# Low parts of eight weight tiles of an MLP made on TensorE instead of VectorE

## The chip, the cores and the metric

The kernel runs on one core of one Trainium2 chip. A core has TensorE (PE: matrix products, with weight loads shown apart as PEld), VectorE (DVE), ScalarE (ACT), GpSimd (POOL) and SyncE (SP), which starts most DMAs. The metric is device time of one execution in microseconds (us).

## The reference

What is computed, in the reference's own words, cut to what matters:

```python
out_up    = np.repeat(softmax_attention(q_d, k_d, v_d), 4, axis=2)   # on means of 4 positions
out_local = softmax(scale * q @ k.T within |i - j| < 4) @ v          # 4 batches, 8 heads, 576 x 64
x = (out_up + out_local) as 2304 tokens x 512
h = x @ w_in;  g = np.maximum(0.01 * h, h);  x = g @ w_out           # first MLP, 512 -> 2048 -> 512
h = x @ w_in2                                                        # second MLP, same sizes
g = where(h >= 1, h, where(h <= -1, 0, (h + 1)**2 / 4));  out = g @ w_out2
```

Weights come with more bits than one 16-bit number holds, and the output has to be as exact as float32.

## The kernel before

**Numbers in two parts.** Each matrix of the MLPs is held as two fp16 matrices, a high part (`hi`) and a low part (`lo`, what the rounding to `hi` left over). A product of two such matrices is three fp16 products (hi·hi, hi·lo, lo·hi) into one PSUM bank.

**Weights.** `weight(m, which, f, due)` prepares one tile of 128x512 of MLP `m` (`which` 0 is `w_in`, 1 is `w_out`; `f` counts 16 tiles of each). A DMA brings the tile; three VectorE operations (`c1`, `c2`, `c3`, lines 611, 617 and 623) put its fp32 words together; ScalarE writes `hi` as fp16, scaled by 256 (line 645); one VectorE operation at line 678 writes `lo` = 256·w − `hi`. Two other ways of making `lo` stand in the code: on TensorE for tiles below `LO_PE` (both zero here, so for none), and by DMA (also none).

**Attention.** It runs ahead of and between the first blocks of the first MLP, until about 140 us, on all engines. Its small fp32 products on TensorE use a part of the 128x128 array each: lines 1118 and 1268 use 64 columns, in pairs of which one writes PSUM partitions 0 to 63 and the other 64 to 127. One fp32 product of the program stands as two MATMUL records in the trace.

**The MLPs.** `stage(m, b)` goes over blocks of 512 or 256 tokens. For a block of 512 tokens one step is 12 products of 128x512 for `h` (`g1`, line 1627), the activation on ScalarE and VectorE (lines 1739, 1763, 1767), and 12 products for the output (`g2`, line 1788 for the first MLP, 1800 for the second). Three blocks of the second MLP use a scheme with fewer products (lines 1656 and 1726). A step needs `w_ready` of its tiles: both parts of the weights.

**What sets the order.** Nothing is scheduled on the chip. `Issue.run` is a planner that runs while the program is built: it gives each operation a cost, keeps a clock, and writes the instructions of each engine in the order in which its plan starts them; each engine then runs its own list in that order. Where the plan leaves TensorE with nothing to do in its first 140 us, `fill` (line 1994) writes in a product of a tile of zeros whose result nobody reads. Such filler products are in the program and are carried out whether or not TensorE would in fact have been idle. A changed cost or operation anywhere in the first 140 us so moves many instructions on every engine, as well as the number of fillers.

Of the kernel before, what the change touches and what calls it, by code (L numbers as in the profile page):

```python
# [56 lines left out]
LO_DMA = {1: (99, 99), 2: (99, 99)}  # L57


LO_PE = (0, 0)  # L60
ADD_PE = ()
PEAK_D = 4500
RESERVE = 2000
# [277 lines left out]
def kernel(  # L341
# [11 lines left out]
    nc = tc.nc  # L353
# [51 lines left out]
    banks = Banks([psum.tile([P, 512], F32, name=f"bank{i}") for i in range(8)])  # L405
# [9 lines left out]
    def t_act(n, psum_src=False, more=0):  # L415
        return (0.051 if psum_src else 0.093) + n / 1200.0 + 0.094 * more
# [9 lines left out]
    def t_mm(n):  # L426
        return 0.003 + n / 2400.0
# [17 lines left out]
    ident_w = const.tile([P, P], F32, name="ident_w")  # L445
    ident_n = const.tile([P, P], F16, name="ident_n")
# [111 lines left out]
    def weight(m, which, f, due):  # L558
        st = {}
        hi, lo = (e[:, f] for e in (w_in, w_out)[which][m])  # L560
        if which == 0:
            hi, lo = (e.rearrange("p c n -> p (c n)") for e in (hi, lo))
# [7 lines left out]
        if second:  # L570
            st = w_two[m, f - 1]
# [75 lines left out]
        free = (lambda: st["f", f].free(),)  # L647
        if m == 1 and f < LO_PE[which]:

            def low():  # L650
                ps = st["ps"] = banks.get()
                nc.tensor.matmul(ps, ident_w, st["f", f].ap, start=True, stop=False)
                nc.tensor.matmul(ps, ident_n, hi, start=False, stop=True)

            ch.op("PE", dict(dur=5 * t_mm(512), cols=5 * 512), low, banks=1, mlp=True,
                  after=free)
            w_ready[m, which, f] = ch.op(
                "ACT", t_act(512, True), lambda: nc.scalar.copy(lo, st["ps"]),
                after=(lambda: banks.put(st["ps"]),))
            ch.close()  # L660
            return
        if LO_DMA[m][0] <= f < LO_DMA[m][1]:

            def neg():
# [6 lines left out]
                after=(lambda: st["n"].free(),))  # L671
# [8 lines left out]
            after=free)  # L680
# [1285 lines left out]
    for m in (1, 2):  # L1966
        b0 = [e[1] for e in ORDER if e[0] == m][0]
        for f in range(KFF):
            i = step_of[m, b0, f // per_step(b0)]
            weight(m, 0, f, i)  # L1970
            weight(m, 1, f, i + 1.5)
# [58 lines left out]
```

## Time and profile before

| | |
|---|---|
| two executions that were timed | 848.5 and 848.83 us (median 848.66) |
| profiled execution, first to last instruction | 847.3 us |
| PE busy | 839.0 us (99%), 5446 MATMUL records |
| DVE busy | 640.7 us (76%) |
| ACT busy | 418.8 us (49%) |
| chain that ended last | PE 97% |

The profiled execution's own time is its span of 847.3 us; the timed ones are 1.2 to 1.5 us longer, which is what lies around the first and last instruction. A MATMUL's record lasts longer than the time until the next one may start (379 ns against some 216 ns for 128x512 fp16), since products overlap in the array; starts, not busy time, tell how fast TensorE goes. Some MATMUL records are missing, so the weight loads (LDWEIGHTS) are the better count.

### The profile page before, as it was taken

Reading aid. Unit: us, or ns where it says so; the run is one execution under the profiler, and the core shown is the slowest. Engines: PE = TensorE matmul, PEld = TensorE weight load, DVE = VectorE, ACT = ScalarE, POOL = GpSimd, SP = SyncE. Lnnn points to the kernel's source line nnn. Section 1 sums busy time; section 2 is a strip of 40 time slices with the busy share of each in tenths; the row PEclk is TensorE's granted clock in tenths of the full one; section 3 lists DMA queues with packets and bytes.
Section 4 is the critical chain, followed back from the end, with each engine's and each line's share of the span. In section 5 each row is a group of like instructions: output and inputs, shape, how many; then the busy total and the mean of one; then the engine's idle time right before and its main releaser. Section 6 shows DMA issues by size and latency. Waiting matters only on the chain.

```text
span 847.3 us, 14367 instructions
## 1 busy us (share of the span) xinstructions
PE 839.0 (99%) x5446; PEld 465.9 (55%) x5458; DVE 640.7 (76%) x1179; ACT 418.8 (49%) x1013; POOL 43.7 (5%) x64
## 2 busy tenths in 40 slices
PE   9999999999999999999999999999999999999997
PEld 5765554444444444444444444444688666666674
DVE  5997999899999899649969989997752446333442
ACT  4888765444444334544444324344533545544553
POOL 2101000000000031100500000000000000000000
PEclk9999999999999999999999999999999999999999
DMA  7779455457720353321842120000000000100010
GB/s 145 167 185 257 154 200 199 149 163 241 197 108 1 110 87 56 79 69 58 134 106 77 54 60 1 0 2 1 1 2 1 1 1 1 50 1 2 1 51 26
DMA packets 76675, 67.76 MB, mean 80 GB/s; under 512 B 36286, under 2 KB 62782, under 8 KB 76606
## 3 DMA queue, kind: packets, MB, share of 16 engines
q1 hardware_dynamic: 65406, 62.69, 25.6%
q0 software_dynamic: 11200, 4.15, 4.3%
q8 instruction: 43, 0.70, 0.4%
q14 instruction: 26, 0.21, 0.1%
HBM read 62.08 MB, written 4.72 MB: 79 GB/s over the span
## 4 chain that ended last, share of the span: by engine, by line
PE 97%; DVE 1%; ACT 1%; issue 0%; ACTq 0%; DVEq 0%
PE bank L1627 32%; PE bank L1788 22%; PE bank L1726 12%; PE bank L1656 11%; PE bank L1800 10%; PE bank L1994 2%; PE bank L923 1%; PE bank L1100 1%; PE bank L1118 1%; PE bank L1049 1%; PE bank L1208 1%; PE bank L1268 1%; PE bank L1251 1%; PE bank L1484 1%; ACT w L1226 0%
## 5 line engine op out<-in xcount | busy, mean ns | idle before, releaser
L1627 PE MATMUL bank<-arena,w 128*128 128x512 f16 (+1 forms) x1344 | 285.6, 364 | 0.0
L1627 PEld LDWEIGHTS <-w 128*128 128x128 f16 x1344 | 130.2, 98 | 135.0 <-issue 1.6
L1788 PE MATMUL bank<-arena,w 128*128 128x512 f16 (+1 forms) x960 | 198.5, 358 | 0.0
L1788 PEld LDWEIGHTS <-w 128*128 128x128 f16 x960 | 93.1, 98 | 88.4 <-issue 0.2
L1767 DVE SCALAR_TENSOR_TENSOR arena<-arena 128x512 f16<-128x512 f32 x144 | 98.9, 687 | 55.5 <-ACT arena L1763 53.9
L1763 ACT ACTIVATE arena<-arena 128x512 f16<-128x512 f32 x144 | 90.6, 629 | 53.7 <-DVE arena L1751 50.2
L1726 PE MATMUL bank<-w,arena 128*128 128x512 f16 x480 | 115.4, 379 | 0.1
L1743 ACT ACTIVATE arena<-bank,half 128x512 f32<-128x512 f32 x72 | 49.5, 687 | 87.3 <-DVE bank L1706 44.4
L1800 PE MATMUL bank<-w,arena 128*128 128x512 f16 x384 | 88.2, 379 | 0.0
L1739 ACT ACTIVATE arena<-bank 128x512 f32<-128x512 f32 x72 | 42.7, 593 | 91.2 <-PE bank L1627 91.0
L1751 DVE SCALAR_TENSOR_TENSOR arena<-arena,bank 128x512 f32<-128x512 f32 x72 | 49.1, 683 | 44.7 <-ACT arena L1747 44.6
L1726 PEld LDWEIGHTS <-arena 128*128 128x128 f16 x480 | 46.2, 98 | 41.7 <-DVE arena L1767 0.6
L1656 PE MATMUL bank<-arena,w 128*128 128x256 f16 (+1 forms) x576 | 62.1, 255 | 0.4 <-DVE bank L1699 0.4
L1800 PEld LDWEIGHTS <-arena 128*128 128x128 f16 x384 | 36.9, 98 | 43.2 <-issue 1.2
L1656 PEld LDWEIGHTS <-w 128*128 128x128 f16 x576 | 49.1, 98 | 13.0 <-issue 0.7
L1656 PE MATMUL bank<-arena 128*128 128x256 f16 (+1 forms) x432 | 46.0, 255 | 0.0
L1747 ACT ACTIVATE arena<-arena 128x512 f32<-128x512 f32 x72 | 45.1, 626 | 1.3
L1656 PEld LDWEIGHTS <-arena 128*128 128x128 f16 x432 | 36.9, 98 | 10.5
L1478 DVE TENSOR_TENSOR arena<-arena 128x768 f32<-128x768 f32 (+2 forms) x60 | 41.2, 688 | 1.4
L1403 DVE TENSOR_TENSOR arena<-arena 128x1792 f32<-128x1792 f32 x20 | 40.3, 2018 | 0.3 <-issue 0.3
L1448 DVE TENSOR_TENSOR arena<-arena 128x1792 f32<-128x1792 f32 x20 | 40.3, 2017 | 0.0
L1411 DVE TENSOR_REDUCE arena<-arena 128x28 f32<-128x1792 f32 x20 | 40.1, 2011 | 0.1
(146 smaller groups left out, 878.1 us busy)
## 6 DMA issues: line engine op xcount, KB each, us to landing
arena<-in_moe_w_in_dram SPq DMA_DIRECT2D x18, 512.0 KB
arena<-in_moe_w_out_dram SPq DMA_DIRECT2D x17, 512.0 KB
w<-in_moe_w_out_dram SPq DMA_DIRECT2D x15, 512.0 KB
out_dram<-arena SPq DMA_DIRECT2D x18, 256.0 KB
arena<-in_moe_w_in_dram SPq DMA_DIRECT2D x4, 1024.0 KB
w<-in_moe_w_in_dram SPq DMA_DIRECT2D x3, 1024.0 KB
arena<-in_k_dram SPq DMA_DIRECT2D x23, 112.0 KB
arena<-in_v_dram SPq DMA_DIRECT2D x23, 112.0 KB
```

Source lines behind the costliest of these rows:

```text
L1478: nc.vector.tensor_tensor(out, x, y, op=ALU.add)
L1627: nc.tensor.matmul(h[:, e], a[:, f, c, :], y[:, :, c, :], start=(n == 0), stop=(n == 3 * KDM - 1),)
L1656: nc.tensor.matmul(o[:, e], a[:, i, c], y[:, k, c, :], start=first and e == 0 and n == 0, stop=n == 5, skip_group_check=True,)
L1726: nc.tensor.matmul(st["acc"][t * NACC // 2 + k], a, y[:, f, :], start=(p == j == e == n == 0), stop=(p == PH - 1 and j == 1 and e == E - 1 ...
L1739: nc.scalar.activation(out=t, in_=st["h", p], func=AF.Prelu, scale=s_in * sg, alpha=0.01)
L1743: nc.scalar.activation(out=t, in_=st["h", p], func=AF.Relu, scale=0.5 * s_in, bias=half)
L1747: nc.scalar.activation(out=t, in_=t, func=AF.Square, scale=s_in ** -0.5)
L1751: nc.vector.scalar_tensor_tensor(out=t, in0=t, scalar=1.0 / s_in, in1=st["h", p], op0=ALU.min, op1=ALU.max)
L1763: nc.scalar.activation(out=gv(p)[0], in_=st["t", p].ap, func=AF.Copy, scale=so)
L1767: nc.vector.scalar_tensor_tensor(out=lo, in0=st["t", p].ap, scalar=so, in1=hi, op0=ALU.mult, op1=ALU.subtract)
L1788: nc.tensor.matmul(o, a, y[:, e, :], start=(first and n == 0 and c % E == 0), stop=(last and n == 2), skip_group_check=True,)
L1800: nc.tensor.matmul(st["acc"][tt], a, y[:, f, :], start=(first and n == 0), stop=(last and n == 2),)
```

## The change

For tiles `f` below 4 of both `w_in` and `w_out` of the first MLP, eight of its 32 tiles, the VectorE operation at line 678 is gone. In its place come, for each of them: two fp32 products of 64 columns of the array each (256·identity times the assembled fp32 words, 512 columns moving), one fp16 product of the full array (−identity times `hi`) that is added in the same bank, and a ScalarE copy of the bank to `lo` as fp16. The dictionary key with `f` keeps the banks of two tiles apart that share `st`.

```diff
-LO_PE = (0, 0)
+LO_PE = (4, 4)
...
             def low():
-                ps = st["ps"] = banks.get()
-                nc.tensor.matmul(ps, ident_w, st["f", f].ap, start=True, stop=False)
-                nc.tensor.matmul(ps, ident_n, hi, start=False, stop=True)
+                ps = st["ps", f] = banks.get()
+                for par in range(2):
+                    pp = slice(par * 64, (par + 1) * 64)
+                    nc.tensor.matmul(
+                        ps[pp], ident_w[:, pp], st["f", f].ap, start=True, stop=False,
+                        skip_group_check=True,
+                    )
+                nc.tensor.matmul(ps, ident_n, hi, start=False, stop=True, skip_group_check=True)
 
             ch.op("PE", dict(dur=5 * t_mm(512), cols=5 * 512), low, banks=1, mlp=True,
                   after=free)
             w_ready[m, which, f] = ch.op(
-                "ACT", t_act(512, True), lambda: nc.scalar.copy(lo, st["ps"]),
-                after=(lambda: banks.put(st["ps"]),))
+                "ACT", t_act(512, True), lambda: nc.scalar.copy(lo, st["ps", f]),
+                after=(lambda: banks.put(st["ps", f]),))
```

The planner writes a new order. From line 666 on, a line's number is 5 higher in the changed kernel. Over the whole program TensorE's list has the eight groups more (lines 654 and 658), and the filler stands 81 times in it instead of 86; all other operations stand as often as before, on every engine. The 81 fillers and the eight groups lie in the stretch of the attention, but the order of the MLPs' steps against each other differs here and there until the end.

TensorE, where the first of the eight groups stands (`ident` is an identity for transposes, `zeros` the filler's tile, `w_61` the room of the second MLP's weights, which serves as a buffer until they come, `w_81` the first MLP's weights). Before:

```order
L1268 MATMUL bank_66<-w_61 64x64 x2
L1268 MATMUL bank_70<-w_61 64x64 x2
L1994 LDWEIGHTS zeros
L1994 MATMUL bank_63<-zeros 128x512
L1100 MATMUL bank_64<-ident,w_61 72x72 x4
L923 MATMUL bank_67<-ident,w_61 128x64 x5
L1100 MATMUL bank_65<-ident,w_61 72x72 x4
L923 MATMUL bank_68<-ident,w_61 128x64 x4
```

and now:

```order
L1273 MATMUL bank_66<-w_61 64x64 x2
L1273 MATMUL bank_70<-w_61 64x64 x2
L1999 LDWEIGHTS zeros
L1999 MATMUL bank_63<-zeros 128x512
L1105 MATMUL bank_64<-ident,w_61 72x72 x4
L654 MATMUL bank_67<-w_61,ident_w 64x512 x2
L658 LDWEIGHTS ident_n
L658 MATMUL bank_67<-w_81,ident_n 128x512
L1105 MATMUL bank_65<-ident,w_61 72x72 x4
```

The group stands between two groups of small products, with no filler taken out beside it.

TensorE again, behind the second step of the first MLP's first block, where two of the groups follow each other, now:

```order
L1632 LDWEIGHTS w_81
L1632 MATMUL bank_65<-arena,w_81 128x512
L654 MATMUL bank_69<-w_61,ident_w 64x512 x2
L658 LDWEIGHTS ident_n
L658 MATMUL bank_69<-w_81,ident_n 128x512
L654 MATMUL bank_70<-w_61,ident_w 64x512 x2
L658 LDWEIGHTS ident_n
L658 MATMUL bank_70<-w_81,ident_n 128x512
L1999 LDWEIGHTS zeros
L1999 MATMUL bank_68<-zeros 128x512
L1999 LDWEIGHTS zeros
L1999 MATMUL bank_68<-zeros 128x512
```

Seven fillers stand behind these two groups, then five transposes and the next step of `g1`. A full-array product stands ahead of each pair and behind it.

ScalarE at the same place, now:

```order
L645 ACTIVATE w_81<-w_61 128x512
L1744 ACTIVATE arena<-bank_65 128x512
L1091 ACTIVATE w_61<-w_61 72x144 x4
L1768 ACTIVATE arena<-arena 128x512
L663 CAST w_81<-bank_69 128x512
L645 ACTIVATE w_81<-w_61 128x512
L663 CAST w_81<-bank_70 128x512
L941 ACTIVATE w_61<-bank_68 128x320
L1744 ACTIVATE arena<-bank_67 128x512
```

The copies (CAST, line 663) stand in ScalarE's one list with `hi` of later tiles, the copies of the attention and the activations of the MLP: while a CAST waits for its bank, all behind it wait too.

## Rows read from the trace of the kernel before

**Rows 1.** The page: span, and busy time, share and instructions of each engine.

```profile
span 847.3 us, 14367 instructions
PE 839.0 (99%) x5446; PEld 465.9 (55%) x5458; DVE 640.7 (76%) x1179; ACT 418.8 (49%) x1013; POOL 43.7 (5%) x64
```

**Rows 2.** The page: the chain that ended last, by engine.

```profile
PE 97%; DVE 1%; ACT 1%; issue 0%; ACTq 0%; DVEq 0%
```

**Rows 3.** PE's waits, longest first: us in total, times, longest.

```profile
PE bank L1994 <- DVE half L451: 1.2, 1, 1.2
PE bank L1049 <- issue: 0.5, 2, 0.3
PE bank L1656 <- DVE bank L1699: 0.4, 1, 0.4
```

**Rows 4.** Timeline of the end: start us, length us, engine and line; the last products.

```profile
834.64 8.37 PE L1726 MATMUL bank<-w,arena 128*128 128x512 f16 x38
```

**Rows 5.** Stretches of 10 us; the first line names the columns.

```profile
core 0: us, PE busy (x) PEld busy (x) DVE busy (x) ACT busy (x) POOL busy (x), PEclk, DMA share, GB/s
20.00:30.00 10.00, 9.49 (x125) 6.79 (x126) 8.50 (x28) 10.00 (x54) 1.48 (x3) 1.00 0.94 163
40.00:50.00 10.00, 9.59 (x133) 7.09 (x134) 9.79 (x34) 8.28 (x32) 0.33 (x4) 1.00 0.80 186
60.00:70.00 10.00, 9.84 (x77) 5.38 (x77) 9.01 (x20) 9.76 (x33) 1.19 (x1) 1.00 0.87 168
130.00:140.00 10.00, 10.00 (x75) 4.89 (x74) 10.00 (x21) 4.38 (x10) 0.00 (x0) 1.00 0.32 102
```

**Rows 6.** Line 1994, the filler: duration ns min/median/max, first and last start.

```profile
L1994 PEld LDWEIGHTS <-zeros x86: 95/98/151, 1.2 to 101.1; 128*128 128x128 bf16 x86
L1994 PE MATMUL bank<-zeros x74: 377/379/634, 1.2 to 101.1; 128*128 128x512 bf16 x74
```

**Rows 7.** Line 1994's share of the first 10 us: PE, then PEld, busy (x).

```profile
0.00:10.00 10.00, 7.77 (x24) 2.73 (x24) 1.00 0.72 133
```

**Rows 8.** PE's timeline about 131 us: full-array steps around one group of line 1118.

```profile
129.13 2.75 PE L1788 MATMUL bank<-arena,w 128*128 128x512 f16 x12
131.81 0.71 PE L1118 MATMUL bank<-w 72*64 72x144 f32 x8
132.46 0.82 PE L1627 MATMUL bank<-arena,w 128*128 128x512 f16 x3
```

**Rows 9.** PE's timeline about 29 us: fillers around a group of line 1268.

```profile
28.40 0.39 PE L1994 MATMUL bank<-zeros 128*128 128x512 bf16 x1
28.72 0.69 PE L1268 MATMUL bank<-w 70*64 70x64 f32 x16
29.34 0.39 PE L1994 MATMUL bank<-zeros 128*128 128x512 bf16 x1
```

**Rows 10.** Lines 1118 and 1268, loads and products: duration ns min/median/max.

```profile
L1118 PE MATMUL bank<-w x64: 286/286/337, 25.9 to 132.2; 72*64 72x144 f32 x64
...
L1268 PEld LDWEIGHTS bank<-w x256: 132/138/138, 28.7 to 135.9; 70*64 70x64 f32 x128
L1268 PE MATMUL bank<-w x256: 222/222/271, 28.7 to 136.0; 70*64 70x64 f32 x128
```

**Rows 11.** Groups of VectorE and ScalarE: busy us, mean ns | idle before, ended by.

```profile
L678 DVE SCALAR_TENSOR_TENSOR w<-w,w 128x512 f16<-128x512 f32 x30 | 20.2, 680 | 0.2
L1739 ACT ACTIVATE arena<-bank 128x512 f32<-128x512 f32 x72 | 42.7, 593 | 91.2 <-PE bank L1627 91.0
L645 ACT ACTIVATE w<-w 128x512 f16<-128x512 f32 x30 | 18.8, 634 | 13.8 <-DVE w L623 13.5
```

**Rows 12.** PE's timeline about 655 us, where it waits in the second MLP.

```profile
654.09 1.76 PE L1726 MATMUL bank<-w,arena 128*128 128x512 f16 x6
656.28 0.81 PE L1656 MATMUL bank<-arena,w 128*128 128x256 f16 x6 [0.43 <-DVE bank L1699]
656.94 1.46 PE L1726 MATMUL bank<-w,arena 128*128 128x512 f16 x6
```

## The prediction

> **What bounds the kernel now.** First the page's busy times: TensorE has 99% of the span, VectorE 76%, ScalarE 49% [rows 1]. A busy TensorE need not be a bound, so next the chain of waits that ended last: 97% of it is TensorE [rows 2]. Then what TensorE waits for: the longest wait is 1.2 us at the very start, all others are under 0.6 [rows 3]. Of the 847.3 us, 8.3 are not PE busy; 1.2 of them are that start and 4.3 lie behind the last product, which ends at 843.0 [rows 4]. So 2.8 us are left between: the program goes as long as TensorE's list of instructions takes.
>
> One thing makes this less plain than it looks. In the first 100 us part of the list is filler, which is carried out whether needed or not: 86 products by their weight loads, 24 of them in the first 10 us [rows 6, 7]. There the stretches show VectorE at 8.5 to 9.8 us of each 10 and ScalarE at up to 10.0 [rows 5]: these two, loaded with attention and weights, decided how much filler the planner put in. Filler is the room in which more TensorE work could be free. But it is free only as far as the new list has fewer fillers, and that is a count: 81 instead of 86.
>
> **VectorE.** Eight operations go, at 0.68 us each [rows 11]: 5.4 us less in a stretch where it is nearly full. As TensorE hardly waits for it outside the start [rows 3], this is worth nothing by itself; what it is worth stands in the five fillers that are gone, 5 x 0.2155 = 1.08 us. The 0.2155 is a full-array product's slot: twelve last 2.75 us from the first start to the last end [rows 8], one lasts 0.379 [rows 6], so (2.75 - 0.379) / 11.
>
> **ScalarE.** Eight copies of a bank come in, at 0.593 by the activation of the same size out of PSUM [rows 11], 4.7 us. ScalarE itself waits for TensorE and VectorE there (91.0 and 13.5 us in front of two of its groups), and TensorE's longest waits are for others [rows 3], so I put the copies at nothing; the cover is the fillers and products that stand between a group and the step that reads its weights. If it is gone, a step waits; that is a rival below.
>
> **TensorE.** Nothing covers this: it is added to the list that is the bound. No row shows a fp32 product of 512 columns, so the price comes from two groups of the same kind, pairs of 64 columns of the array.
>
> - *Rate.* Line 1118 has 8 records of 144 columns in 0.71 us [rows 8], and its last record lasts 0.286 [rows 10]: seven steps from start to start in 0.424, 0.0606 each, or 0.42 ns for a column of a record. Line 1268 has 16 records of 64 columns, (0.69 - 0.222) / 15 = 0.0312, or 0.49 ns [rows 9, 10]. A product has two records, so it is 0.84 to 0.98 ns for a column of a product, on average over the two products of a pair that go side by side. Ours are longer than either, so nearest to line 1118, whose start is shared by more columns: 2 x 512 x 0.842 = 0.862 us. The other end is 2 x 512 x 0.975 = 0.998.
> - *Going over and back.* In rows 8 the twelfth product before the group ends its columns at 129.13 + 12 x 0.2155 = 131.716 and the next step starts at 132.46: 0.744 us, of which 4 products x 144 columns x 0.842 ns are 0.485. So 0.259 us go to the two changes between the full array and the halves, and to the first loads. The same sum on line 1268 (28.40 + 0.2155 to 29.34, 0.724 us, less 8 x 64 x 0.842 = 0.431) leaves 0.293 [rows 9], so it isn't chance. I take 0.259; the low end is nothing, for a group that stands beside other half-array products (the first stands between transposes, the next two between full-array ones).
> - *The fp16 product* is an ordinary one: 0.2155.
>
> One group: 0.862 + 0.259 + 0.2155 = 1.337 us, eight: **10.7 us**. Ends: 8.6 without any changing over (8 x 1.077), 11.8 at line 1268's rate (8 x 1.472).
>
> **The later order.** The steps of the second MLP stand a little differently against each other. The one place there where TensorE waits for another engine costs 0.43 us, with some tenths more hidden in the steps before it: six products last 1.76 instead of 1.46 [rows 12]. I add 0.4 for one more such wait; ends: -0.4, when the old one goes, and +2, for several.
>
> **The sum.** 10.7 - 1.1 + 0.4 = +10.0 us. The profiled execution would span 857.3 instead of 847.3; the two timed executions are 848.66 in the middle, 1.36 above that span, so **858.7 us**, +1.2%. With the ends of its terms: 8.6 - 1.1 - 0.4 = +7.1 (855.8) to 11.8 - 1.1 + 2 = +12.7 (861.4). The clock stays: granted 1.00 of 2.4 GHz in each stretch [rows 5], and TensorE has no less to do.
>
> **A rule against it.** In rows 10 a weight load of line 1268 lasts 138 ns while records start every 31 ns: the loads lie beside products, although both halves of a pair use the same rows of the array. The Trainium skill (TensorE: Matmul & The Clock Gate, Part 3, "What overlaps and what doesn't") says that a weight load overlaps with products in flight only when the row groups differ, which is not so in our pairs. By that rule each group would show its loads; this trace disagrees, with the 138 ns against 31. The mechanism stays as a rival, since our loads belong to products six times as long.
>
> **Rivals.**
>
> - *The loads show.* Four loads of 0.138 a group, 8 x 0.55 = 4.4 us on top: 863.1. Rows 9 and 10 speak against it. 0.04.
> - *The halves don't go side by side* when the columns are 512. Then a column costs 2 x 0.842 ns: 1.724 + 0.259 + 0.2155 = 2.20 a group, 17.6 us in all, 17.6 - 1.1 + 0.4 = +16.9: 865.6. For it: such long pairs are in no row. Against: in rows 8, one after the other, 4 x 144 x 1.684 would be 0.97 us, and the whole detour took 0.744. 0.04.
> - *ScalarE becomes the wait.* A CAST stands in ScalarE's one list behind activations and ahead of `hi` of the next tile, and the next step needs it. From 40 to 50 us ScalarE is busy 8.3 of 10, from 60 to 70 us 9.8 [rows 5]. If each of the eight copies comes late by its own length, 8 x 0.593 = 4.7: 863.4; if `hi` (0.634) behind it is late too, 8 x 1.227 = 9.8: 868.5. It decides where the copy needs more than the fillers behind the group give; behind the third and fourth these are seven, 1.5 us, against 0.593 + 0.634 + 0.593 = 1.82 for copy, `hi`, copy. For it: exactly that. Against: TensorE also has the transposes there, and in the rows of before ScalarE waits for others, 13.5 us ahead of line 645 for VectorE alone [rows 11]. 0.07 for the smaller price, 0.03 for the larger.
> - *Not slower.* VectorE is the true limit of the first 60 us, and what it gives up pulls the MLP forward while the eight groups go into room that was filler. The fillers behind the first 10 us are 86 - 24 = 62, 62 x 0.2155 = 13.4 us, more than the groups' 10.7: if all fell away, 848.66 + 10.7 - 13.4 = 846. It decides at 50 fillers fewer; the list has 5 fewer, and what else TensorE could win is the 2.8 us of gaps. 0.02.
>
> That the change doesn't do what it says is excluded by the list: eight groups stand in it and eight operations of VectorE don't.
>
> **How the numbers follow.** My forecast has 0.80, the rivals 0.20. The range, 855.5 to 864, holds the forecast's ends, the visible loads and ScalarE's smaller price, and leaves out the halves in turn, ScalarE's larger price and no loss, 0.09, with some for what I didn't think of. A measurement of this kernel tells about 2%, or 17 us, from no change. Faster by that much needs 831.7, which no case gives: 0.01. Slower needs 865.6: the halves in turn stand right there and ScalarE's larger price is above it; 0.07 with something for stalls that add up. Within 2%: 0.92.
>
> **What will show it.** Right: line 654 with 32 records, those of one half about 0.43 us apart and the two halves within some 10 ns of each other; a group from the product before to the product behind about 1.3 us; 81 loads of the filler; the steps of the first MLP behind 100 us all later by about the same; PE's waits still short. Wrong: starts of line 654 in a row, 0.43 us apart one by one; a wait of PE on line 663 or of ScalarE on line 654 followed by one of PE; steps that are not later at 140 us but later at the end.

## The result, and the profile after

The changed kernel takes 859.2 us (858.98 and 859.43) against 848.66: a ratio of 1.0125, 95% interval 1.0095 to 1.0154. The forecast was 858.7. The profiled execution spans 857.6 instead of 847.3 us, 10.3 more.

The page of the changed kernel, first lines and chain of waits, to be held against [rows 1] and [rows 2]:

```profile
span 857.6 us, 14404 instructions
PE 850.9 (99%) x5493; PEld 467.5 (55%) x5493; DVE 637.3 (74%) x1171; ACT 421.9 (49%) x1021; POOL 44.1 (5%) x64
PE 96%; DVE 2%; ACT 1%; issue 0%; ACTq 0%; DVEq 0%
```

TensorE is busy 11.9 us longer, in part because twelve of the filler's MATMUL records are missing before (74 for 86 loads [rows 6]) and none after (81 for 81); VectorE is busy 3.4 us less, and the chain is TensorE's as before. The groups, by their lines in the changed kernel (duration ns min/median/max, first and last start; the last row is the filler's loads):

```profile
L654 PEld LDWEIGHTS bank<-w,ident_w x32: 132/136/138, 45.1 to 96.5; 128*64 128x64 f32 x32
L654 PE MATMUL bank<-w,ident_w x32: 591/594/644, 45.1 to 97.0; 128*64 128x512 f32 x32
L658 PE MATMUL bank<-w,ident_n x8: 389/390/390, 46.1 to 97.5; 128*128 128x512 f16 x8
L663 ACT CAST w<-bank x8: 577/586/597, 46.5 to 97.9; 128x512 f16<-128x512 f32 x8
L1999 PEld LDWEIGHTS <-zeros x81: 95/98/152, 1.2 to 101.0; 128*128 128x128 bf16 x81
```

Two groups that follow each other, in PE's timeline of the changed kernel; their price can be read off as in [rows 8]:

```profile
62.04 0.81 PE L1632 MATMUL bank<-arena,w 128*128 128x512 f16 x3
62.78 1.08 PE L654 MATMUL bank<-w,ident_w 128*64 128x512 f32 x4
63.79 0.39 PE L658 MATMUL bank<-w,ident_n 128*128 128x512 f16 x1
64.11 1.08 PE L654 MATMUL bank<-w,ident_w 128*64 128x512 f32 x4
65.12 0.39 PE L658 MATMUL bank<-w,ident_n 128*128 128x512 f16 x1
65.35 1.03 PE L1999 MATMUL bank<-zeros 128*128 128x512 bf16 x4
```

From the start of one group's first half to that of the next it is 64.11 - 62.78 = 1.33 us. Four records of 0.59 us in 1.08 us can only lie side by side: two start 7 ns apart, the other two 0.48 us later (0.43 us in one of the eight groups).

Where the 10.3 us lie is told by the first and last start of `g1`'s products, before and after:

```profile
L1627 PE MATMUL bank<-arena,w x1344: 272/379/390, 56.1 to 638.1; 128*128 128x512 f16 x165, 128*128 128x256 f16 x27
```

```profile
L1632 PE MATMUL bank<-arena,w x1344: 272/379/390, 57.5 to 647.4; 128*128 128x512 f16 x165, 128*128 128x256 f16 x27
```

The first step starts 1.4 us later. Two groups and five fillers fewer (59 loads of the filler instead of 64 ahead of that step) make 2 x 1.33 - 5 x 0.2155 = 1.6. The two executions were not level before that, though. The first 18 fillers of before, the same of the changed kernel, and its filler at 28 us, which is at 28.40 before [rows 9]:

```profile
1.20 6.30 PE L1994 MATMUL bank<-zeros 128*128 128x512 bf16 x18 [1.20 <-DVE half L451]
1.20 5.62 PE L1999 MATMUL bank<-zeros 128*128 128x512 bf16 x18 [1.20 <-DVE half L451]
27.91 0.39 PE L1999 MATMUL bank<-zeros 128*128 128x512 bf16 x1
```

TensorE's list is the same up to the first group, at 45 us. In each execution the first fillers start 0.43 us apart and the later ones 0.2155, and this one left the slow pace earlier; so it was 0.5 us ahead. From 28 us on the first step is 1.9 us later, and the whole span 10.8.

From the first to the last of these products it is 589.9 instead of 582.0 us, 7.9 more; six groups are 8.0, and the fillers there are 22 in both kernels. The last 1.0 us comes behind it, 0.7 of it at three places in the second MLP. Two of them in PE's timeline:

```profile
735.90 1.46 PE L1731 MATMUL bank<-w,arena 128*128 128x512 f16 x6
737.46 1.47 PE L1661 MATMUL bank<-arena 128*128 128x256 f16 x12
...
739.42 1.46 PE L1731 MATMUL bank<-w,arena 128*128 128x512 f16 x6
740.71 0.82 PE L1661 MATMUL bank<-arena,w 128*128 128x256 f16 x6
...
746.11 2.17 PE L1731 MATMUL bank<-w,arena 128*128 128x512 f16 x8
```

Six products and their successor are 1.29 us apart at 739.42 and 1.56 at 735.90; the eight at 746.11 last 2.17 us where 1.89 would do (seven slots and 0.379). Other waits are still short:

```profile
PE bank L1999 <- DVE half L451: 1.2, 1, 1.2
PE bank L1661 <- DVE bank L1704: 0.4, 1, 0.4
PE bank L1256 <- DVE w L1238: 0.2, 1, 0.2
```

### The profile page after: what moved, and what is told of

It is laid out like the page before. It is cut to its first block, busy times and chain, and to the rows that moved or that the text cites. A ratio compares the mean times of both kernels' runs of the same rounds, so it can differ in the third digit from the quotient of the medians.

```text
span 857.6 us, 14404 instructions
## 1 busy us (share of the span) xinstructions
PE 850.9 (99%) x5493; PEld 467.5 (55%) x5493; DVE 637.3 (74%) x1171; ACT 421.9 (49%) x1021; POOL 44.1 (5%) x64
## 4 chain that ended last, share of the span: by engine, by line
PE 96%; DVE 2%; ACT 1%; issue 0%; ACTq 0%; DVEq 0%
PE bank L1632 32%; PE bank L1793 22%; PE bank L1731 11%; PE bank L1805 10%; PE bank L1661 9%; PE bank L1999 2%; PE bank L928 1%; PE bank L1123 1%; PE bank L1213 1%; PE bank L1054 1%; PE bank L1273 1%; PE bank L1105 1%; PE bank L1256 1%; PE bank L654 1%; PE bank L1489 1%
```

## Experiments

Two theories stand against each other. One: TensorE's list is the bound, so each piece that is added counts in full. The other: VectorE and ScalarE set the pace of the first 100 us, and what TensorE does there is in part room. The kernel before took 849.0 to 849.1 us beside these runs. The changed kernel's 859.2 was measured beside 848.66, so a difference against it is sure to some 0.4 us only.

**TensorE's part alone.** In the kernel before, at eight places of TensorE's list:

```diff
+                    if e == "PE" and self.extra and t >= self.extra[0] and self.banks.free:
+                        self.extra.pop(0)
+                        self.dummy(self.banks.free[0])
...
+            nc.tensor.matmul(
+                ps[pp].rearrange("p (a n) -> p a n", a=4), ident_w[:, pp], wide,
+                start=True, stop=False, skip_group_check=True,
+            )
...
+    sch.extra, sch.dummy = [42.2, 48.1, 58.4, 59.5, 66.5, 74.6, 89.0, 90.1], dummy
```

`extra` holds the plan's times for the eight groups; of `dummy`, which writes one, a product of the halves is shown.

> TensorE's part of the change alone: the kernel before in its own order with all 86 fillers and VectorE's eight low parts as they were, and eight groups of the changed kernel's form (two fp32 halves of 512 columns, one fp16 product) written into TensorE's list about where the changed kernel has them, on constants, with a result that nobody reads. Theory (TensorE's list is full, so what is added counts in full): 8 x 1.33 = 10.7, 849.0 + 10.7 = 859.7. Rival (the other engines need the time that the list has, so that an added piece is in part absorbed as a removed one was given back in part, 4.2 of 9.0 us without the pairs): 849.0 + 5 = 854.

Measured 859.11 (858.27 to 859.73), ratio 1.012 (1.0107 to 1.0133): +10.1 us, nearly the whole of the change's 10.5, with VectorE's work, the fillers and the order as before and without the copies. First and last start of `g1`'s products and all of PE's waits in that run:

```profile
L1630 PE MATMUL bank<-arena,w x1344: 272/379/390, 58.3 to 647.8; 128*128 128x512 f16 x165, 128*128 128x256 f16 x27
```

```profile
PE bank L1997 <- DVE half L454: 1.2, 1, 1.2
PE bank L1659 <- DVE bank L1702: 0.4, 1, 0.4
```

The list moved back by 10.1 of the 10.7 us that eight groups take, so next to nothing took them up. This is the run that shows the mechanism.

**VectorE's part alone**, in the kernel before:

```diff
-            "DVE", t_dve(512), lambda: nc.vector.scalar_tensor_tensor(
+            "DVE", t_dve(512), lambda: nc.vector.memset(lo, 0.0) if m == 1 and f < 4
+            else nc.vector.scalar_tensor_tensor(
```

> VectorE's part of the change alone, nearly: the kernel before in its own order, with a fill of zeros (0.27 us for this many bytes) in place of each of the eight operations of line 678 (0.68 us); the low parts of these tiles are left out of the computation. VectorE has 8 x 0.41 = 3.3 us less to do. Theory (TensorE's list doesn't wait for it): 849.0. Rival (VectorE sets the pace beside TensorE: giving it 5.4 us back in the changed kernel cost 1.9): 849.0 - 1.2 = 847.8, or all of it, 845.7.

Measured 849.43 (848.41 to 852.77, 12 runs), ratio 1.001 (1.000 to 1.0019). A fill takes 0.27 us where the operation takes 0.68, so VectorE is spared 3.3 us here, not the change's 5.4; they are worth nothing in that order.

**VectorE's work put back** in the changed kernel:

```diff
+            if m == 1 and f < LO_PE[which]:
+                nc.vector.scalar_tensor_tensor(
+                    out=lo, in0=st["f", f].ap, scalar=SW, in1=st["f", f].ap,
+                    op0=ALU.mult, op1=ALU.subtract,
+                )
```

> The changed kernel, in the same order, with an operation of line 683's form and size put back on VectorE behind the third of each of the eight tiles (its result is overwritten by ScalarE's copy): VectorE has its 5.4 us again, TensorE keeps the groups. Theory (VectorE is not what TensorE's list waits for): 859.2 to 860. Rival (what VectorE gave up was pulling TensorE forward): up to 8 x 0.68 = 5.4 more, 864.6.

Measured 861.07 (860.67 to 861.57), 1.9 above the changed kernel's 859.2 (1.5 if each is held against its own kernel before): neither. An order that was written with a lighter VectorE doesn't carry the heavier one for nothing, though about a third of 5.4 us is all that comes through. The operation stands right behind the third of its tile, not behind `hi` as line 678 did; what it would cost there isn't shown.

**The pair left out** of the changed kernel:

```diff
-                for par in range(2):
-                    ... (the two fp32 products)
-                nc.tensor.matmul(ps, ident_n, hi, start=False, stop=True, skip_group_check=True)
+                nc.tensor.matmul(ps, ident_n, hi, start=True, stop=True)
```

> The changed kernel with the two fp32 products of each of the eight groups left out of TensorE's list, and everything else in the same order: the fp16 product alone writes the bank, ScalarE copies it as before (lo is then only -hi: this part of the computation is left out). Theory (TensorE's list is the bound and a group is 1.33 us of it): 8 x (1.33 - 0.2155) = 8.9 us less than the changed kernel's 859.2, so 850.3. Rival (ScalarE's copies and their waits make the loss): all eight copies are still there, so 858 to 859.5.

Measured 856.34, from 853.39 to 858.5; the two longer runs have a mean granted clock of 0.99. The profiled one spans 853.5, 4.1 less than the changed kernel, after a late start: its filler at 28 us is at 29.00, 1.1 later. From there it is 5.2 less, so 3.7 of the 8.9 us that TensorE was spared don't come out. That filler, then two stretches (columns as in [rows 5]) and the longest wait:

```profile
29.00 0.39 PE L1993 MATMUL bank<-zeros 128*128 128x512 bf16 x1
70.00:80.00 10.00, 10.00 (x69) 5.27 (x68) 5.45 (x14) 7.00 (x25) 1.31 (x3) 1.00 1.19 212
80.00:90.00 10.00, 8.29 (x63) 4.16 (x62) 8.72 (x22) 6.62 (x22) 1.18 (x1) 1.00 0.76 221
```

```profile
PE bank L1626 <- DVE w L677: 1.7, 1, 1.7
```

A step of `g1` now comes to its weights before VectorE has made them (line 677 there is the low part of another tile). Neither theory had this: the list is full, but not far behind it stand the others, so taking away stops paying soon, while adding always costs.

**One product of the full array** for the two halves:

```diff
-                for par in range(2):
-                    ... (the two fp32 products)
+                nc.tensor.matmul(ps, ident_w, st["f", f].ap, start=True, stop=False)
```

> The changed kernel with one fp32 product of the full array in place of the two halves, in the same order. Theory (0.26 us of each group are the two changes between full array and halves, and the passes cost 0.86 in either form): 8 x 0.26 = 2.1 us less than 859.2, so 857.1. Rival (changing over costs nothing, it is all passes): 859.2. Rival (a full fp32 product is dearer than two halves side by side, by as much again): 8 x (0.86 - 0.26) = 4.8 more, 864.

Measured 858.75 (858.73 to 859.18), the profiled run 856.9 against 857.6. The two groups of above in PE's timeline:

```profile
62.83 0.59 PE L1627 MATMUL bank<-arena,w 128*128 128x512 f16 x2
63.26 1.02 PE L652 MATMUL bank<-w,ident_w 128*128 128x512 f32 x2
64.12 0.38 PE L653 MATMUL bank<-w,ident_n 128*128 128x512 f16 x1
64.33 1.02 PE L652 MATMUL bank<-w,ident_w 128*128 128x512 f32 x2
```

A group is 64.33 - 63.26 = 1.07 us instead of 1.33, so the 0.26 for going over and back are there as priced, and the passes cost the same 0.86 in either form. Of the 2.1 us only 0.5 to 0.7 seem to reach the end. Its `g1` starts at 58.1, later than the changed kernel's 57.5 though two shorter groups lie ahead:

```profile
L1627 PE MATMUL bank<-arena,w x1344: 272/379/390, 58.1 to 646.7; 128*128 128x512 f16 x165, 128*128 128x256 f16 x27
28.62 0.39 PE L1994 MATMUL bank<-zeros 128*128 128x512 bf16 x1
```

The second line, the filler that the changed kernel starts at 27.91, tells why: 0.7 us were lost at the start, ahead of every group. Without that some 1.4 us are saved. From the first step on 588.6 us instead of 589.9: 1.3, near the 1.55 of six groups. Behind the first step the list rules; the two groups ahead of it gave 0.1 or 0.2 of their 0.5 us, which isn't settled.

**The order alone**, without the groups and the copies:

```diff
-                nc.tensor.matmul(... the three products of a group ...)
+                pass
...
-                "ACT", t_act(512, True), lambda: nc.scalar.copy(lo, st["ps", f]),
+                "ACT", t_act(512, True), lambda: nc.vector.scalar_tensor_tensor(
+                    out=lo, in0=st["f", f].ap, scalar=SW, in1=hi, op0=ALU.mult, op1=ALU.subtract),
```

> The changed kernel's order with the eight groups and the eight copies taken out again, and lo made by VectorE at the place where the copy stood in the plan: what the new order and the five missing fillers do without the groups. Theory: 5 fillers x 0.2155 = 1.1 less than before, and about 0.7 more for waits of TensorE in the second MLP that the changed kernel's trace has and the one of before has not: 848.3; the groups are then 859.2 - 848.3 = 10.9. Rival (the new order itself costs, and the groups lie partly in room): 851 to 856.

Measured 859.02 (858.1 to 859.39), as if the groups cost nothing. The stretches say why this is no answer (columns as in [rows 5]: the third number from the end is the granted clock):

```profile
40.00:50.00 10.00, 8.75 (x113) 6.56 (x113) 9.71 (x34) 8.44 (x33) 0.10 (x1) 0.95 0.77 184
50.00:60.00 10.00, 10.00 (x92) 6.91 (x92) 6.07 (x17) 4.62 (x22) 1.47 (x3) 0.50 0.90 203
60.00:70.00 10.00, 10.00 (x35) 4.06 (x35) 6.62 (x17) 6.90 (x24) 1.19 (x1) 0.69 0.70 148
```

TensorE was idle 1.25 us between 40 and 50, and then ran at 0.50 of its clock, the 1.2 GHz level, into the next stretch. By the clock alone 0.5 + 5.0 + 3.1 = 8.6 us of full speed are missing in these three rows; 859.0 - 8.6 = 850.4 is an estimate of the order without that. What the order does by itself stays open.

**Sixteen tiles** (`LO_PE = (8, 8)`):

> The change for 8 tiles of each matrix, sixteen in all. The planner writes another order: 74 fillers instead of 86. Theory (every group is added to the list): 16 x 1.33 - 12 x 0.2155 + 0.5 = +19.2, so 867.9. Rival (ScalarE becomes the wait as copies add up): over 872. Rival (later groups stand in room that VectorE's lighter load makes): below 863.

Measured 868.17 (867.69 to 868.63), ratio 1.0225 (1.0209 to 1.024), +19.1 against +19.2 expected, over the double of the groups. The price holds, and among PE's waits none is for a copy.

**Without filler.** In `fill`, in both kernels, first for all behind 10 us of the plan, then for those behind 50:

```diff
         to = (spare or banks.free)[:1]
+        if t > 10.0:          # 50.0 in the second pair
+            return bool(to)
```

> The kernel before, same order, with the 58 fillers behind the first 10 us not written into TensorE's list; everything computed. If the list alone is the bound: 58 x 0.2155 = 12.5 us less, 836.2. If the fillers stand where TensorE would wait for VectorE and ScalarE: 848.7. Theory: the second in the main, since VectorE is busy 8.5 to 9.8 us of each 10 there; 845 to 849. If the clock falls in the gaps, longer than that.

> The changed kernel, same order, with its 53 fillers behind the first 10 us not written in. Beside the kernel before without its fillers this tells whether the eight groups would find room among TensorE's waits once no filler stands there. Theory (they stand where TensorE has work or where the next step waits for them): 9 to 11 us longer than the kernel before without fillers. Rival (the room is there and filler hides it): less than 5 us longer than that kernel.

Measured 859.35 (852.01 to 860.47) and 856.94 (855.21 to 858.01). Three stretches of the first:

```profile
20.00:30.00 10.00, 9.09 (x82) 6.67 (x80) 6.84 (x19) 8.13 (x40) 1.47 (x3) 0.63 0.81 146
40.00:50.00 10.00, 10.00 (x97) 7.53 (x93) 6.80 (x25) 6.53 (x32) 0.00 (x0) 0.50 0.39 89
60.00:70.00 10.00, 10.00 (x88) 7.34 (x86) 8.11 (x25) 8.15 (x36) 0.00 (x0) 0.65 0.55 124
```

The granted clock is 0.50 at 40 to 50 us and below 0.7 in the stretches from 20 and from 60, and the kernel before becomes 10 us longer with 12.5 us less in its list. That the clock could fall was named; the forecast of 845 to 849 was wrong. The pair can't be compared for the groups, since the clock was lost in different stretches.

> The kernel before, same order, without its 25 fillers behind 50 us of the plan; the 61 before it stay and hold the clock while the attention is alone. If each filler is time of the list: 25 x 0.2155 = 5.4 less, 843.6. If they stand where TensorE would wait: 849.0. Theory (TensorE and the other engines need nearly the same time, so about half comes back as waits, as without the pairs): 846.5, which would be faster than both kernels.

> The changed kernel, same order, without its 24 fillers behind 50 us of the plan. List alone: 24 x 0.2155 = 5.2 less, 854.0; waits: 859.2; half: 856.6. Beside the kernel before with the same fillers left out it tells whether the groups find room once filler doesn't stand there and the clock is kept: if the groups cost what they take, 9 to 11 us longer than that kernel; if the room was there, less than 6.

Measured 848.52 (845.55 to 849.48, ratio 0.9988, 0.998 to 0.9997) and 854.59 (1.0072, 1.0059 to 1.0085). In the kernel before, leaving 25 fillers out gains 0.5 us of 5.4. What came in their place, in its stretches and waits:

```profile
70.00:80.00 10.00, 7.97 (x69) 4.46 (x66) 6.65 (x18) 8.48 (x35) 1.31 (x3) 0.93 1.05 256
80.00:90.00 10.00, 10.00 (x86) 5.46 (x85) 9.42 (x23) 8.08 (x28) 1.31 (x3) 0.90 0.72 228
```

```profile
PE bank L1788 <- ACT w L645: 1.1, 1, 1.1
PE bank L1193 <- ACT w L936: 0.9, 1, 0.9
PE bank L1100 <- ACT arena L1763: 0.6, 1, 0.6
```

TensorE is idle for 2 us between 70 and 80, and the clock falls behind that, 0.93 and 0.90 in the two stretches. So the 0.5 us have the clock in them. Of its eleven executions one kept a mean clock of 1.00, and it took 845.55 us, 3.4 less than the kernel before; the others have 0.995 to 0.998. In the changed kernel the clock stayed, at 0.999 or 1.00 in all five, and 24 fillers are worth 4.6 of their 5.2.

The 6.1 us between the two medians (854.59 - 848.52) are therefore not the price of the groups without the late fillers. With the clock kept in both it is 854.59 - 845.55 = 9.0 us, which rests on one execution and fits the theory's 9 to 11: the groups find little room even where no filler stands.

## Why the prediction was right

- *The list is the bound, an added group counts in full.* Right: +10.1 for the groups alone (10.7 by their price), +19.1 for sixteen, and six groups behind the first step are 7.9 us there.
- *The price, 1.337 us.* Measured 1.33. The rate of line 1118 was the right one of the two ends: 0.43 us for 512 columns of a record. The changes between halves and full array are 1.33 - 1.07 = 0.26, against 0.259.
- *The sum.* +10.3 in the profiled span, against +10.0. The later order was set at 0.4; the second MLP's waits are 0.7, and 0.3 more lies in the end. The early start hid 0.5 us, so the list's part is nearer to 10.8. From span to time 1.36 us were added, out of different executions; the execution of 859.43 us spans 857.6, which is 1.8. That 858.7 came within 0.5 us of 859.2 is in part luck: the other two misses made the forecast too low, and the early start hid as much again.
- *VectorE's 5.4 us are worth nothing.* Right for the kernel before as far as it was put to the test, 3.3 of the 5.4 us (849.43 against 848.99). In the changed order putting them back costs 1.9.
- *Five fillers fewer, 1.1 us.* It fits the start of the first step roughly: 1.4 later, or 1.9 from 28 us on, where 1.6 was due. But a filler is not always a slot: in the kernel before 25 of them are worth 0.5 us, or 3.4 with the clock kept, in the changed one 24 are worth 4.6.
- *The loads show; the halves go in turn.* Neither: loads of 136 ns, starts 7 ns apart.
- *ScalarE becomes the wait.* No: TensorE waited nowhere of note for line 663. One reason given was misread: the 91.0 us in front of line 1739 are of the whole program, and only 1.2 of them lie ahead of 105 us, where the copies are.
- *Not slower.* It fell by the count, as argued. Even without its 24 late fillers the changed kernel, at 854.59, stays above the kernel before with all of its own.
- What the argument had too simple is that the list being full was read as room on all other engines. It is so when something is added. When something is taken out, what comes back ran from 0.5 of 5.4 us (the kernel before without its late fillers; 3.4 with the clock kept) over some 5 of 8.9 (the pair) to 4.6 of 5.2 (the changed kernel without its late fillers); the rest turns to waits or, where TensorE idles, to a lower clock.

## What to carry to other kernels

Where one engine's list is full because a planner padded it, ask for each edit whether it adds or removes: added work costs its whole length, removed work pays only up to the next engine's finish. Price an unseen instruction by the nearest row of its kind, rate and change-over apart, and count what the new program really holds: padding that is left in is paid for too (4.6 us here), as long as the clock stays without it. Hold two profiles against each other where their lists are still the same, before you read tenths out of them. When you take work out to test its price, look at the granted clock first.

## What the runs showed of the hardware

- A fp32 product of the full array (two records) takes 0.86 us for 512 columns (63.26 to 64.12 in the run with one product). A pair of fp32 products of 64 columns, side by side, takes no longer but for 0.26 us, 1.33 against 1.07 for the group, which is what [rows 8] gave for going over and back.
- In the run of the order alone, idle time of 1.25 us in one stretch of 10 us was followed by the lower clock, 0.50, in the next, and it stayed there although TensorE's records then filled the stretch. Where the pair was left out, 1.71 us of idle time between 80 and 90 us in the profiled run had no lower clock with it: it stayed at 1.00. With 58 fillers out the kernel before took 10 us more, so these, 0.2155 us each, were worth more than they cost; the 24 late ones of the changed kernel were not.
- The first fillers start 0.43 us apart, twice the later 0.2155, with 1.00 in the clock column. When that ends differs from one execution to the next: the same 18 fillers take 5.62 us in the profile of the changed kernel and 6.30 in that of the kernel before. What ends it isn't shown.
